# q and k transposed in float32 and split on the way out of PSUM, scores of two heads as 64-row tiles side by side, products with v in one piece

## The chip, the cores and the metric

The kernel is one program on one core of a Trainium2 chip. The metric is device time in microseconds (us) of one execution, from which medians over several runs are taken. Six instruction streams matter: TensorE (PE for matmuls, PEld for its weight loads), VectorE (DVE), ScalarE (ACT), GpSimd (POOL) and SyncE (SP), which here only issues DMAs. Each stream runs its instructions in program order; streams wait for each other through semaphores.

## What is computed

Attention with a learned bias, and behind it a mixture of experts. Cut to what matters here (B = 8, H = 8, S = 576, D = 64):

```python
scores = (1 / sqrt(D)) * np.matmul(q, k.transpose(0, 1, 3, 2))
psi_rel = np.log1p(np.abs(pos[:, None] - pos[None, :]))
x = (psi_rel / np.log1p(np.maximum(pos[:, None], 1.0)))[..., None]
bias = np.maximum(x @ w1 + b1, 0.0) @ w2              # S x S x H
scores = scores + bias.transpose(2, 0, 1)[None]
attn = np.exp(scores - scores.max(-1)); attn = attn / attn.sum(-1)
x = np.matmul(attn, v)                                # then, per token:
e = argmax(x @ w_gate + modality_bias); y = gate * (relu(x @ w1[e]) @ w2[e])
```

The matrix products have to be nearly float32. The kernel gets this from fast products of a reduced type (F32R) by splitting a number into a high part (its value rounded to F32R) and a low part (the rest), and adding the products high·high, low·high and high·low.

## The kernel before

**Stages.** First a table of the bias is made (`bias_table`, with `bias_hidden`, `bias_out`, `bias_put`): 36 blocks, each a hidden layer on DVE or ACT, a matmul with `w2` on PE, a scaling on the way out of PSUM, and DMAs that lay the rows out in `NBm` (query rows below 512) and `NBr` (the last 64). The last four blocks (`bias_late`) run inside the first pair of heads, and their rows go to `NBr` in 32 DMAs (L211). `first_steps` puts the preparation of pair 0 and 1 between the blocks. Then comes attention, and then the experts' tiles (from about 700 us on), which the change does not touch.

**Attention** goes through 32 pairs of heads (`attention`, L566), one pair after the other, and each pair through five steps u = 0 to 4. Step u handles the query rows of chunk u (128 rows of each head for u below 4; for u = 4 the last 64 rows of both heads together). What each step issues, and in which order, stands in the five strings of `ORDER` (L558): each letter is a piece of work, and since no scheduler reorders anything, the letters set the order on every engine at once.

- `S` (`scores`): the products of a chunk of q with all 576 keys, into one of two PSUM tiles `sps` (one per head); behind it on DVE one custom instruction (L435) that adds the bias, finds the minimum and writes `E`. Before, one `S` is one head of a chunk ("slot"): 128-row matmuls, in which the 128 rows hold high and low part of q over the 64 dimensions, four of 288 columns each. The scores come out negated.
- `e`, `f` (`exps`): exp of head 0 and head 1 on ACT, in place in `E`.
- `t`, `T` (`etrans`): four PE transposes each of `E` of the chunk two steps earlier (head 0, head 1) into PSUM `eps`, and the copy out to `eT` by `take` (on ACT for the names in `ON_ACT`, otherwise on DVE).
- `C` (`compact`, POOL) and `R` (`rtrans`): the last 64 keys of each chunk, copied together and transposed into `rT`.
- `a A` and `b c` (`av`): products of v with `eT` for query half 0 and half 1 of the pair before, each half in two parts; the second part adds the product for the last 64 keys (L517) and copies out to `xTb` on ACT.
- `k q` (`split`, POOL): high and low part of q and k in SBUF, side by side in the free dimension. `0` to `4` (`prep`): PE transposes of these, so that high parts land in rows 0 to 63 and low parts in rows 64 to 127 of `QT` and `KT`, and the copies out. `W` (`swap`): two DMAs that write `QT` once more with its halves exchanged. `K` (`heads`): four DMAs that put the parts for u = 4 into `KH` and `QD`. `L`, `V`: loads for later pairs.
- `X`, `B`: steps of the routing of the batch before, on PE and other engines.

All DMAs of this stage but the routing's scatters stand in one queue in the order of SP's instructions.

## Time and profile before

| | us |
|---|---|
| runs | 1196.64, 1191.96, 1195.97; median 1195.97 |
| the profiled execution | 1198.66 |
| its span, from first to last instruction | 1196.7 |
| first score matmul / last score matmul | 71.1 / 698.4 |
| PE busy in the span | 1132.1 |
| ACT / DVE / POOL busy in the span | 728.3 / 754.1 / 383.7 |

The page of the profile gives busy times and the costliest groups, each line of kernel.py with its engine, the tiles it writes and reads, the count, the busy time, and the idle time just before with what ended it. The timeline gives instructions in order of time: start, duration, engine, line, operation, how many were merged into the row, and in square brackets the idle time before the row with its releaser. A row of windows gives the busy time of each engine in a stretch, then the clock granted to TensorE (1.00 is full), the share of the DMA engines and GB/s. All times count from the start of the span.

### The profile page before, as it was taken

The page shows a single profiled execution, that of the slowest core. Times are in us where ns is not written, and L with a number is a line of the kernel's source. Part 1 is how long each engine was busy: PE and PEld are TensorE (multiplying, and loading weights), DVE is VectorE, ACT ScalarE, POOL GpSimd, SP SyncE. Part 2 cuts the span into 40 slices and gives each one's busy share as a digit, 9 for nine tenths or more (in the row PEclk, how much of TensorE's full clock was granted, in tenths as well). Part 3 has the DMA queues.
Part 4 walks back from the last instruction along what each step waited for, and adds up shares of the span by engine and source line. Part 5 has one row for each costly group of instructions (what it writes and reads, how often), then busy time and mean ns, then how long its engine had stood idle before and what let it go on. Part 6 is the DMA issues. An engine that isn't in the chain of part 4 may idle for free. (4 is left out here: it accounts for less than half of the span.)

```text
span 1196.7 us, 23090 instructions
## 1 busy us (share of the span) xinstructions
PE 1132.1 (95%) x8202; PEld 919.5 (77%) x8202; DVE 754.1 (63%) x1552; ACT 728.3 (61%) x1412; POOL 383.7 (32%) x525
## 2 busy tenths in 40 slices
PE   7977999899999899999998979999999999999997
PEld 3445777667778577777776758988899899989975
DVE  7974567457666475666757637577555645664667
ACT  5565667657767477677775654545545645554566
POOL 2203223434435325444353323532221123122122
PEclk9998999999999999999999999999999999999999
DMA  6854433764745635555365560221113314311361
GB/s 173 192 121 126 112 95 102 115 94 111 125 96 126 98 93 125 113 121 125 93 116 111 162 108 10 72 67 37 45 55 115 107 45 144 113 45 48 121 244 33
DMA packets 91311, 124.26 MB, mean 104 GB/s; under 512 B 35697, under 2 KB 60657, under 8 KB 91188
## 3 DMA queue, kind: packets, MB, share of 16 engines
q1 hardware_dynamic: 83188, 101.35, 36.3%
q0 software_dynamic: 8000, 21.35, 5.9%
q8 instruction: 68, 1.11, 0.5%
q14 instruction: 55, 0.45, 0.1%
HBM read 140.09 MB, written 19.90 MB: 134 GB/s over the span
## 5 line engine op out<-in xcount | busy, mean ns | idle before, releaser
L435 DVE CUSTOM_DVE_ANT_0 Eb<-sps,NBm 128x576 f32<-128x576 f32 x256 | 190.1, 755 | 183.8 <-PE sps L420 93.7
L449 ACT ACTIVATE Eb<-Eb,mn 128x576 f32<-128x576 f32 x288 | 221.5, 770 | 40.5 <-DVE mn L435 36.7
L420 PE MATMUL sps<-KT,QT 128*128 128x288 f32 x1152 | 222.7, 319 | 22.0 <-DMA QT<-QT 21.1
L420 PEld LDWEIGHTS sps<-KT,QT 128*128 128x128 f32 x1152 | 166.5, 191 | 27.4 <-issue 22.3
L1144 PE MATMUL p<-QT,w1hi 128*128 128x256 f32 x1152 | 163.9, 285 | 5.2 <-ACT w1hi L1117 5.2
L463 PE MATMUL eps<-idf,Eb 128*128 128x128 f32 x1024 | 159.9, 282 | 0.6 <-DVE lgs L781 0.3
L507 PE MATMUL xps<-eT,vraw 128*64 128x288 f32 x1024 | 155.0, 425 | 1.5 <-DVE QT L1129 1.0
L1144 PEld LDWEIGHTS p<-QT,w1hi 128*128 128x128 f32 x1152 | 150.8, 194 | 7.3 <-ACT w1hi L1117 6.1
L463 PEld LDWEIGHTS eps<-idf,Eb 128*128 128x128 f32 x1024 | 114.9, 142 | 39.5 <-issue 29.5
L1170 POOL DMA_INDIRECT out<-mo,idt x36 | 51.8, 1440 | 291.1 <-ACT mo L1169 262.6
L1147 DVE SCALAR_TENSOR_TENSOR hl<-p,hh 128x512 fp32r<-128x512 f32 x72 | 49.7, 690 | 138.9 <-ACT hh L1146 134.6
L454 POOL COPY rem<-Eb 128x128 f32<-128x128 f32 x128 | 37.5, 297 | 252.3 <-ACT Eb L449 245.1
L309 ACT ACTIVATE eT<-eps 128x512 f32<-128x512 f32 x192 | 111.4, 591 | 9.5 <-PE eps L463 8.7
L1161 PE MATMUL p<-w2lo,hh 128*128 128x512 f32 x288 | 112.9, 392 | 3.5 <-DVE w2lo L1111 2.2
L1111 DVE TENSOR_TENSOR w2lo<-NBm,w2hi 128x1024 fp32r<-128x1024 f32 x81 | 98.7, 1224 | 24.9 <-ACT w2hi L1110 24.8
L1161 PE MATMUL p<-w2hi,hh 128*128 128x512 f32 x288 | 114.0, 396 | 0.0
L1161 PE MATMUL p<-w2hi,hl 128*128 128x512 f32 x288 | 112.5, 391 | 0.0
L1146 ACT ACTIVATE hh<-p 128x512 fp32r<-128x512 f32 x72 | 43.1, 598 | 111.2 <-PE p L1144 103.1
L309 ACT ACTIVATE xTb<-xps 128x288 f32<-128x288 f32 x64 | 26.4, 412 | 122.9 <-PE xps L517 118.8
L507 PEld LDWEIGHTS xps<-eT,vraw 128*64 128x64 f32 x1024 | 63.1, 138 | 46.6 <-issue 12.6
L1111 DVE TENSOR_TENSOR w1lo<-NBm,w1hi 128x1024 fp32r<-128x1024 f32 x84 | 97.9, 1227 | 0.0
L1144 PE MATMUL p<-QT,w1lo 128*128 128x256 f32 x576 | 93.4, 285 | 0.3 <-DVE w1lo L1118 0.3
(227 smaller groups left out, 1991.3 us busy)
## 6 DMA issues: line engine op xcount, KB each, us to landing
NBm<-moe_w SPq DMA_DIRECT2D x24, 2048.0 KB
NBm<-moe_w SPq DMA_DIRECT2D x46, 1024.0 KB
QT<-QT SPq DMA_DIRECT2D x64, 304.0 KB
NBm<-xTb SPq DMA_DIRECT2D x32, 288.0 KB
KH<-KT SPq DMA_DIRECT2D x64, 144.0 KB
qraw<-q SPq DMA_DIRECT2D x32, 256.0 KB
kraw<-k SPq DMA_DIRECT2D x32, 256.0 KB
vraw<-v SPq DMA_DIRECT2D x32, 256.0 KB
```

The costliest lines, as they stand in the source:

```text
L309: self.nc.scalar.activation(out, ps, AF.Copy, scale=scale)
L420: nc.tensor.matmul(ps[:, half, :], q, k[:, HS * half : HS * half + HS], start=i == 0, stop=i == len(terms) - 1, skip_group_check=True,)
L435: nc.vector.tensor_tensor_reduce(out=e.rearrange("p (t w) -> p t w", t=2), in0=ps, in1=nb.rearrange("p (t w) -> p t w", t=2), scale=1.0, s ...
L449: self.nc.scalar.activation(e, e, AF.Exp, bias=mn, scale=-1.0, accum_out=sm)
L463: nc.tensor.transpose(ps[:, k, :], e[:, part, P * k : P * k + P], self.idf)
L507: nc.tensor.matmul(ps[o, :], v[:, h, k, :], self.eT[:, h, k, sl], start=k == 0, stop=False, tile_position=(0, 64 * h), skip_group_check=True,)
L1111: (lo or self.nc.vector).tensor_tensor(l, w, h.bitcast(F32), op=ALU.subtract)
L1144: nc.tensor.matmul(ps[:, a, :], w[:, c, fs], x[:, c, :], start=i == 0, stop=i == len(ops) - 1)
L1146: nc.scalar.activation(hh[:, sl, :], ps, AF.Relu)
L1147: nc.vector.scalar_tensor_tensor(hl[:, sl, :], ps, 0.0, hh[:, sl, :].bitcast(F32), op0=ALU.max, op1=ALU.subtract)
L1161: nc.tensor.matmul(ps, h[:, f, sl], m[:, f, :], start=i == 0, stop=i == len(ops) - 1)
L1170: nc.gpsimd.indirect_dma_start(out=self.out, out_offset=IndirectOffsetOnAxis(ap=ids, axis=0), in_=o, in_offset=None, bounds_check=self.n_t ...
```

## The change

**q and k.** The POOL split, the F32R identity and the DMAs `W` and `K` go. `prep` now transposes the raw float32 q and k, both heads side by side (head 0 lands in rows 0 to 63, head 1 in rows 64 to 127), four 128x128 transposes for q (`0`), four for k (`1`) and two small ones for the last 64 rows (`2`), instead of 18. Out of PSUM, ACT writes the high part and DVE then subtracts it from the PSUM value and writes the low part, so `QT` and `KT` hold the high parts in plane 0 and the low parts in plane 1. `D` copies the block-diagonal `QD` on POOL. The loads of q and k bring the heads of a chunk next to each other, in pieces of 64 numbers.

**Scores.** One `S` now does both heads of a chunk. For each of three terms (high·high, low·high, high·low) and each half of the keys it issues two matmuls of 64 rows, head 0 at array rows 0 to 63 and head 1 at rows 64 to 127, into two different PSUM tiles: 12 matmuls where two slots had 8. u = 4 keeps six 128-row matmuls.

**v.** `a A` and `b c` stand together, and the copies out are letters of their own (`y`, `z`).

**Order.** The strings of `ORDER` are rewritten. **Bias.** The last 64 rows are grouped another way, with a small table `tg1` of their own, so that `NBr` is written by 8 DMAs instead of 32.

```diff
@@ bias_put
-            for cg in range(4):
-                for par in range(2):
-                    r0 = 64 * par + 4 * cg + c
-                    nc.sync.dma_start(self.NBr[r0 : r0 + 49 : 16, :, :], o[32 * cg + par : 32 * cg + 32 : 2, :])
+            r0 = 16 * (blk - NMAIN)
+            for par in range(2):
+                nc.sync.dma_start(self.NBr[64 * par + r0 : 64 * par + r0 + 16, :, :], o[par:P:2, :])
@@ qk_loads
-            nc.sync.dma_start(
-                t[:, 0:8, :].rearrange("p (h c) d -> p h (c d)", h=2),
-                src[:, 0:512, :].rearrange("h (p c) d -> p h (c d)", c=4),
-            )
+            for h in range(2):
+                nc.sync.dma_start(t[:, h:8:2, :], src[h, 0:512, :].rearrange("(p c) d -> p c d", c=4))
+                yield
+            nc.sync.dma_start(t[0:64, 8:10, :], src[:, 512:S, :].rearrange("h r d -> r h d"))
             yield
-            for h in range(2):
-                nc.sync.dma_start(t[64 * h : 64 * h + 64, 8, :], src[h, 512:S, :])
-                yield
@@ prep
+        raws = (self.qraw[n], self.kraw[n])
+        if part < 2:
+            for c in range(4):
+                x = raws[part][:, 2 * c : 2 * c + 2, :].rearrange("p h d -> p (h d)")
+                nc.tensor.transpose(ps[:, P * c : P * c + P], x, self.idf)
         else:
+            for j, x in enumerate(raws):
+                x = x[0:64, 8:10, :].rearrange("p h d -> p (h d)")
+                nc.tensor.transpose(ps[:, 64 * j : 64 * j + 64], x, self.idf[0:64, 0:64])
...
         def out():
+            for j in (0, 1) if part == 2 else (part,):
+                cols = slice(512, S) if part == 2 else slice(0, 512)
+                p = ps[:, 64 * j : 64 * j + 64] if part == 2 else ps
+                T = (QT, KT)[j]
+                hi, lo = T[:, 0, cols], T[:, 1, cols]
+                if j == 0:
+                    nc.scalar.activation(hi, p, AF.Copy, scale=sc)
+                    nc.vector.scalar_tensor_tensor(lo, p, sc, hi.bitcast(F32), op0=ALU.mult, op1=ALU.subtract)
+                else:
+                    nc.scalar.copy(hi, p)
+                    nc.vector.tensor_tensor(lo, p, hi.bitcast(F32), op=ALU.subtract)
-    def swap(self, n):
...
     def heads(self, n):
-            self.nc.sync.dma_start(KH[o, :], KT[0:64, h, :])
-            self.nc.sync.dma_start(QD[o, o], QT[0:64, 0, 512 + P * h : 576 + P * h])
+            self.nc.gpsimd.tensor_copy(self.QD[o, :, o], QT[o, 0:2, 512:S].bitcast(F32))
@@ scores
+        sps = [t[:, :, 0:HS] for t in self.sps]
+        terms = ((0, 0), (1, 0), (0, 1))
+        for i, (a, b) in enumerate(terms):
             for half in range(2):
+                k = KT[:, b, HS * half : HS * half + HS]
+                kw = dict(start=i == 0, stop=i == len(terms) - 1, skip_group_check=True)
+                if u == 4:
+                    nc.tensor.matmul(sps[1][:, half, :], self.QD[:, a, :], k, **kw)
+                    continue
+                for h in range(2):
+                    o = slice(64 * h, 64 * h + 64)
+                    q = QT[o, a, P * u : P * u + P]
+                    nc.tensor.matmul(sps[h][:, half, :], q, k[o], tile_position=(64 * h, 0), **kw)
@@ av
-        if part == 1:
-            self.take(f"av{half}", self.xT[n][:, sl], ps)
+    def av_out(self, n, half):
+        self.take(f"av{half}", self.xT[n][:, HS * half : HS * half + HS], self.avps[half][:, 0:HS])
@@ ORDER
-        "S R S e f k X T a t B C",
-        "L S 1 A t e S 4 f 0 C T",
-        "t S S e f b q C T",
-        "B S c e S T 3 2 t f W C V",
-        "S X X e K T B X t",
+        "S R T e X t f B C",
+        "L S T e a A t y f 0 D C",
+        "S t e T f 1 C",
+        "B S e b c T z f 2 t C V",
+        "S X X e T B X t",
```

The change in three places, in the order in which instructions stand on an engine. On DVE, from the last bias instruction of u = 1 on in one pair; L435 is the scores' instruction (its second row reads the minimum out), `QT` and `KT` from L313 and L311 are copies out of `prep`, `eT` from L311 those of the transposed `E`. Before:

```order
L435 ISA Eb,mn_3_1253<-sps_750,NBm 128x576
L435 ISA mn_3_1253 128x1
L313 TENSOR_SCALAR QT_73<-xps_78 128x2x64
L313 TENSOR_SCALAR QT_73<-xps_77 128x512
L435 ISA Eb,mn_4_1279<-sps_749,NBm 128x576
L435 ISA mn_4_1279 128x1
L435 ISA Eb,mn_5_1285<-sps_750,NBm 128x576
L435 ISA mn_5_1285 128x1
L311 COPY eT<-eps_752 128x4x128
L435 ISA Eb,mn_6_1306<-sps_749,NBm 128x576
```

With the change the same place reads as follows (L418 is the scores' instruction, L378 and L381 write the low parts of q and k, L314 is `take`):

```order
L418 ISA Eb,mn_11_1196<-sps_728,NBm 128x576
L418 ISA mn_11_1196 128x1
L378 SCALAR_TENSOR_TENSOR QT_73<-xps_77,QT_73 128x512
L418 ISA Eb,mn_20_1240<-sps_727,NBm 128x576
L418 ISA mn_20_1240 128x1
L418 ISA Eb,mn_21_1242<-sps_728,NBm 128x576
L418 ISA mn_21_1242 128x1
L314 COPY eT<-eps_730 128x4x128
L381 TENSOR_TENSOR KT_105<-xps_78,KT_105 128x512
L418 ISA Eb,mn_30_1276<-sps_727,NBm 128x576
```

The instructions ahead of the scores of u = 2 and u = 3 now read `QT` and `KT` as well as PSUM: they come behind ACT's copy of the high part, not behind PE alone.

On ACT at the same place (L449 exp, L309 `take`), before:

```order
L309 ACTIVATE xTb_94<-xps_78 128x288
L309 ACTIVATE eT<-eps_751 128x4x2x64
L449 ACTIVATE Eb,sums_1184<-Eb,mn_2_1230 128x576
L309 ACTIVATE KT_109<-xps_78 128x2x64
L449 ACTIVATE Eb,sums_1184<-Eb,mn_3_1253 128x576
L309 ACTIVATE rT<-eps_752 128x64
```

and with the change, from the exp of u = 1, head 0, on (L433 exp, L312 `take`, L377 the high part of q):

```order
L433 ACTIVATE Eb,sums_1150<-Eb,mn_10_1194 128x576
L312 ACTIVATE eT<-eps_729 128x4x2x64
L312 ACTIVATE xTb_94<-xps_78 128x288
L433 ACTIVATE Eb,sums_1150<-Eb,mn_11_1196 128x576
L377 ACTIVATE QT_73<-xps_77 128x512
L312 ACTIVATE eT<-eps_729 128x4x128
```

The high part of q is new on ACT and stands behind the copies of `eT` and `xTb` and behind the exp of head 1.

On PE, around the products with v for half 0 of one pair (L463 and L469 transposes of `E`, L507 and L517 products with v, L369 transposes of q), before:

```order
L463 MATMUL eps_752<-idf,Eb 128x128 x4
L507 MATMUL xps_78<-eT,vraw_1346 64x288 x4
L463 MATMUL eps_751<-idf,Eb 128x128 x4
L420 MATMUL sps_749<-KT_108,QT_72 128x288 x4
L369 MATMUL xps_77<-idr,qs 128x128 x4
L507 MATMUL xps_78<-eT,vraw_1346 64x288 x4
L517 MATMUL xps_78<-rT,vrem_117 128x288
L469 MATMUL eps_751<-idf,Eb 128x128 x4
L420 MATMUL sps_750<-KT_108,QT_72 128x288 x4
```

and with the change, from the last score matmul of u = 1 to the first of u = 2 (L409 scores, L458 and L453 transposes of `E`, L491 and L501 products with v, L363 transposes of q):

```order
L409 MATMUL sps_728<-KT_105,QT_73 128x288
L458 MATMUL eps_730<-idf,Eb 64x64 x2
L491 MATMUL xps_78<-eT,vraw_1115 64x288 x8
L501 MATMUL xps_78<-rT,vrem_109 128x288
L453 MATMUL eps_729<-idf,Eb 128x128 x4
L363 MATMUL xps_77<-idf,qraw_1174 128x128 x4
L409 MATMUL sps_727<-KT_105,QT_73 128x288
```

The two parts of a half stand together with nothing between, and score matmuls, which before lay between them, come before and behind.

More of the change, by code (lines that the diff above doesn't have):

```diff
@@ L41 @@
 NBLK = S4 // 4
-X0 = 131
-TW = X0 + S4
+X0, X1 = 115, 15
+TW, TW1 = X0 + S4, X1 + S4
 def bias_base(blk, cg):
@@ L53, in bias_base @@
         return o + 16 * cg + 64 * half, c
-    return P + cg, blk - NMAIN
+    return P + 4 * (blk - NMAIN) + cg, 0
 def bias_rows(blk, cg):
     s, c = bias_base(blk, cg)
-    return [4 * (s + 4 * g) + c for g in range(4)]
+    return [4 * (s + 4 * g) + c if blk < NMAIN else 4 * s + g for g in range(4)]
 def n_tiles(n_tok):
@@ L274, in attn_early @@
         self.rt = right(name="rt", bufs=1)
-        self.idr = cp.tile([P, P], F32R, name="idr")
-        nc.scalar.copy(self.idr, self.idf)
         self.eT = cp.tile([P, 2, 4, S], F32, name="eT")
         self.rT = cp.tile([P, S], F32, name="rT")
-        self.qs = cp.tile([P, 9, 2, D], F32R, name="qs")
-        self.ks = cp.tile([P, 9, 2, D], F32R, name="ks")
         self.KT = [cp.tile([P, 2, S], F32R, name=f"KT{k}") for k in range(2)]
-        self.KH = cp.tile([P, S], F32R, name="KH")
-        self.QD = cp.tile([P, P], F32R, name="QD")
+        self.tg1 = cp.tile([P, 4, TW1], F32, name="tg1")
+        self.QD = cp.tile([P, 2, P], F32R, name="QD")
         nc.gpsimd.memset(self.QD.bitcast(F32), 0.0)
@@ L349, in load_v @@
         self.vmain[n] = t
-    def split(self, n, part):
-        x = (self.qraw, self.kraw)[part].pop(n)
-        xs = (self.qs, self.ks)[part]
-        self.nc.gpsimd.tensor_copy(xs[:, :, 0, :], x)
-        self.nc.gpsimd.tensor_tensor(xs[:, :, 1, :], x, xs[:, :, 0, :].bitcast(F32), op=ALU.subtract)
     def prep(self, n, part):
@@ L364, in prep @@
         ps = self.xbank()
-        pr = ps.bitcast(F32R).rearrange("p (j w) -> p j w", j=4)
-        if part < 4:
-            xs = (self.qs, self.ks)[part // 2]
-            for j in range(4):
-                nc.tensor.transpose(
-                    pr[:, j, :], xs[:, 4 * (part % 2) + j, :, :].rearrange("p a d -> p (a d)"), self.idr
-                )
-        else:
-            for j, xs in enumerate((self.qs, self.ks)):
-                nc.tensor.transpose(pr[:, j, :], xs[:, 8, :, :].rearrange("p a d -> p (a d)"), self.idr)
+        raws = (self.qraw[n], self.kraw[n])
@@ L407, in scores @@
+    def scores(self, n, u):
         nc = self.nc
-        b, p = divmod(n, NP)
+        p = n % NP
         QT, KT = self.QT[n % 2], self.KT[n % 2]
-        ps = self.sps[slot % 2 if slot < 8 else 1][:, :, 0:HS]
-        if slot < 8:
-            c, h = divmod(slot, 2)
-            o = (704 if h else 0) + P * c
-            terms = [(QT[:, sw, o : o + P], KT[:, h, :]) for sw in range(2)]
-        else:
-            c = 4
-            terms = [(QT[:, 1, 512 + 64 * h : 640 + 64 * h], KT[:, h, :]) for h in range(2)] + [(self.QD, self.KH)]
@@ L418, in scores @@
-        for i, (q, k) in enumerate(terms):
-            for half in range(2):
-                nc.tensor.matmul(
-                    ps[:, half, :],
-                    q,
-                    k[:, HS * half : HS * half + HS],
-                    start=i == 0,
-                    stop=i == len(terms) - 1,
-                    skip_group_check=True,
-                )
-        if slot == 0:
-            self.sums[n] = self.smp.tile([P, 9], F32, tag="sums", name=f"sums{n}", bufs=8)
-        if slot in (0, 2, 4, 6, 8):
-            self.E[n, c] = self.Eb[:, next(self.e_next)]
@@ L432, in scores @@
-        e = self.E[n, c][:, slot % 2, :]
-        nb = self.NBm[:, 8 * c + 2 * p + slot % 2, :] if slot < 8 else self.NBr[:, p, :]
-        mn = self.smp.tile([P, 1], F32, tag="mn", name=f"mn{n}_{slot}", bufs=4)
-        nc.vector.tensor_tensor_reduce(
-            out=e.rearrange("p (t w) -> p t w", t=2),
-            in0=ps,
-            in1=nb.rearrange("p (t w) -> p t w", t=2),
-            scale=1.0,
-            scalar=3.0e38,
-            op0=ALU.add,
-            op1=ALU.min,
-            accum_out=mn,
-        )
@@ new lines, in scores @@
+        if u == 0:
+            self.sums[n] = self.smp.tile([P, 9], F32, tag="sums", name=f"sums{n}", bufs=8)
+        self.E[n, u] = self.Eb[:, next(self.e_next)]
+        found = []
+        for h in range(2 if u < 4 else 1):
+            e = self.E[n, u][:, h, :]
+            nb = self.NBm[:, 8 * u + 2 * p + h, :] if u < 4 else self.NBr[:, p, :]
+            mn = self.smp.tile([P, 1], F32, tag="mn", name=f"mn{n}_{u}{h}", bufs=4)
+            nc.vector.tensor_tensor_reduce(
+                out=e.rearrange("p (t w) -> p t w", t=2),
+                in0=sps[h if u < 4 else 1],
+                in1=nb.rearrange("p (t w) -> p t w", t=2),
+                scale=1.0,
+                scalar=3.0e38,
+                op0=ALU.add,
+                op1=ALU.min,
+                accum_out=mn,
+            )
+            found.append((e, mn, self.sums[n][:, 2 * u + h : 2 * u + h + 1]))
@@ L537, in first_steps @@
         add(0, lambda: self.load_v(0))
-        add(2, lambda: self.split(0, 0))
-        add(4, lambda: self.split(0, 1))
-        for blk, k in zip(self.PREP0, (0, 1, 4, 2, 3)):
+        for blk, k in zip(self.PREP0, range(3)):
             add(blk, lambda k=k: pe(k))
             add(blk + 1, lambda k=k: evac.pop(k)())
-        add(self.SWAP0, lambda: self.swap(0))
-        add(self.HEADS0, lambda: self.heads(0))
         if self.n_pair > 1:
```

66 lines of the change are left out of this document (30 added, 36 removed).

## Prediction

> **What bounds the kernel now.** I read the page first, then windows over the attention stage, then the waits of PE there, then the timeline of one pair.
>
> ```profile
> PE 1132.1 (95%) x8202; PEld 919.5 (77%) x8202; DVE 754.1 (63%) x1552; ACT 728.3 (61%) x1412; POOL 383.7 (32%) x525
> ```
>
> The average says PE. The windows say how strictly: two stretches of four pairs (one batch) each.
>
> ```profile
> 448.14:522.82 74.68, 74.34 (x588) 58.58 (x588) 48.66 (x132) 53.01 (x127) 32.44 (x53) 1.00 0.52 116
> 522.82:597.50 74.68, 74.33 (x588) 58.56 (x588) 48.69 (x132) 53.01 (x127) 32.43 (x53) 1.00 0.52 116
> ```
>
> The columns are PE, PEld, DVE, ACT, POOL, the clock, the DMA share, GB/s. Both take 74.68 us to the last digit, PE is busy all but 0.34 us, the clock is full: a quiet pair takes 74.68 / 4 = **18.67 us** and PE alone sets it. ACT has 53.0 of 74.7 us, DVE 48.7. Outside such stretches PE waits:
>
> ```profile
> PE sps L420 <- DMA QT<-QT: 21.1, 4, 13.9
> PE xps L374 <- POOL ks L356: 4.2, 2, 3.0
> PE xps L491 <- POOL rem L454: 3.6, 1, 3.6
> PE xps L491 <- issue: 1.5, 1, 1.5
> ...
> 60.00:100.00 40.00, 24.14 (x233) 16.64 (x230) 23.09 (x57) 20.46 (x43) 5.13 (x8) 0.85 0.55 133
> ...
> 226.00:232.00 6.00, 4.08 (x33) 3.07 (x31) 2.23 (x5) 3.88 (x10) 3.63 (x7) 1.00 0.64 131
> 236.00:246.00 10.00, 7.02 (x38) 5.36 (x37) 3.42 (x9) 4.29 (x12) 4.38 (x7) 0.66 0.74 88
> 408.00:420.00 12.00, 9.16 (x65) 6.30 (x65) 2.79 (x9) 4.79 (x10) 4.06 (x9) 0.86 0.40 91
> 636.00:646.00 10.00, 6.78 (x47) 4.56 (x48) 7.45 (x28) 4.12 (x10) 4.12 (x9) 0.83 0.56 124
> 678.00:688.00 10.00, 7.93 (x50) 6.39 (x52) 2.75 (x8) 5.40 (x12) 4.16 (x7) 0.83 0.48 137
> ```
>
> The first four rows are waits of PE from 60 to 735 us (total, times, longest). The windows show what each long one costs besides: the clock falls behind it. A window's loss is its length by one minus the clock: 6.0 us, 0, 3.4, 1.7, 1.7 and 1.7.
>
> **Stalls that the change takes away.** The longest is the first, between pair 0 and 1:
>
> ```profile
> 71.22 13.25 SPq L211 DMA_DIRECT2D NBr<-xTb  x23
> 83.95 5.67 SPq L211 DMA_DIRECT2D NBr<-xTb  x10
> 98.26 0.82 PE L420 MATMUL sps<-KT,QT 128*128 128x288 f32 x2 [13.91 <-DMA QT<-QT]
> ```
>
> SP issues 32 small DMAs for `NBr` in 18.4 us (0.57 each), only then the loads and the swap that pair 1 waits for. Eight issues of the same kind are about 8 x 0.6 = 5 us from 72 on, over before PE's wait began at 84 (98.26 - 13.91), and no swap is left. So 21.1 us of waits for swaps and 4.2 us for POOL's split go, and with them the clock losses behind them, 6.0 + 3.4 + 1.7 + 1.7 = 12.8 us: **38 us**. The two waits for `rem` (5.1 us, and 1.7 of clock) may stay: POOL still stands behind the routing's scatters. POOL loses its split, but a lap with less slack (below) will feel the scatters more often, for which I give back 4. Net **34 us**.
>
> **PE's own work in a pair.** All from one pair, by starts of groups:
>
> ```profile
> 488.13 0.66 PE L463 MATMUL eps<-idf,Eb 128*128 128x128 f32 x4
> 488.72 1.19 PE L507 MATMUL xps<-eT,vraw 128*64 128x288 f32 x8
> 489.84 0.66 PE L463 MATMUL eps<-idf,Eb 128*128 128x128 f32 x4
> 490.25 0.78 PE L420 MATMUL sps<-KT,QT 128*128 128x288 f32 x4
> 490.53 0.60 ACT L309 ACTIVATE eT<-eps 128x512 f32<-128x512 f32 x1 [0.33 <-PE eps L463]
> ...
> 491.20 0.76 DVE L435 CUSTOM_DVE_ANT_0 Eb<-sps,NBm 128x576 f32<-128x576 f32 x1 [2.31 <-ACT eT L309]
> ...
> 492.38 0.75 PE L517 MATMUL xps<-rT,vrem 128*128 128x288 f32 x2
> 492.96 0.60 PE L469 MATMUL eps<-idf,Eb 128*128 128x128 f32 x4
> ...
> 495.15 1.10 PEld L420 LDWEIGHTS sps<-KT,QT 128*128 128x128 f32 x8
> 495.18 1.30 PE L420 MATMUL sps<-KT,QT 128*128 128x288 f32 x8
> ...
> 501.25 0.89 PE L369 MATMUL xps<-idr,ks 128*128 128x128 f32 x8
> 501.96 0.63 PE L463 MATMUL eps<-idf,Eb 128*128 128x128 f32 x4
> ```
>
> A 288-column score matmul: eight weight loads in 1.10, (1.10 - 0.19) / 7 = 0.13 us each, and 0.133 fits the matmuls. A transpose of float32 takes 0.109 (L469: four in 0.60 with the last lasting 0.27), so four 0.44; one of F32R (0.71 / 8) 0.089. A v step, both heads' records side by side: 1.19 for four, the last lasting 0.43, first one slow, so 0.243. From 488.13 to 490.25 are 2.12 us; two times 0.44 and 4 x 0.243 are 1.85, so going into column tiles and out again costs 0.27, about 0.145 a change. L517 takes 0.58, 0.68 with the change before it.
>
> Scores: 32 matmuls x 0.133 = 4.26 us give way to 24 steps of two matmuls. That two 64-row tiles run side by side no row shows; the nearest is the pair of column tiles in L507. I take 0.133 a step: 3.19, so 1.07 less. Bounds: 0.12 (a tenth less) and 0.266 (one after the other). Transposes: 18 x 0.089 = 1.6 to about 1.1, 0.5 less. Changes of tile: before there are five segments of column tiles in a pair (a, A, b, c and the small transposes L474), ten changes; after, four row segments and two column segments of which two pairs touch, again ten. v in one piece thus gains nothing by itself, it pays for the score tiles. PE's work falls by 1.5 us, to 17.1 with routing, 16.1 without (routing steps are about 1 us a pair). By PE alone that is 32 x 1.5 = 48 us.
>
> **What is late next.** In the new order each low part waits on DVE for ACT's high part, and the scores' instruction queues behind it. Hops, from these rows and the ones above:
>
> ```profile
> 496.09 0.76 DVE L435 CUSTOM_DVE_ANT_0 Eb<-sps,NBm 128x576 f32<-128x576 f32 x1 [0.27 <-issue]
> ...
> 496.77 0.75 DVE L435 CUSTOM_DVE_ANT_0 Eb<-sps,NBm 128x576 f32<-128x576 f32 x1
> ...
> 498.30 0.69 DVE L311 COPY eT<-eps 128x512 f32<-128x512 f32 x1 [0.76 <-PE eps L463]
> ...
> 498.90 0.75 DVE L435 CUSTOM_DVE_ANT_0 Eb<-sps,NBm 128x576 f32<-128x576 f32 x1
> ...
> 500.56 0.41 ACT L309 ACTIVATE xTb<-xps 128x288 f32<-128x288 f32 x1 [2.04 <-PE xps L517]
> ...
> 500.87 0.77 ACT L449 ACTIVATE Eb<-Eb,mn 128x576 f32<-128x576 f32 x1
> ...
> 501.63 0.59 ACT L309 ACTIVATE eT<-eps 128x512 f32<-128x512 f32 x1
> ...
> 502.17 0.60 ACT L309 ACTIVATE KT<-xps 128x512 fp32r<-128x512 f32 x1
> ...
> 503.56 0.76 DVE L435 CUSTOM_DVE_ANT_0 Eb<-sps,NBr 128x576 f32<-128x576 f32 x1 [0.17 <-ACT Eb L449]
> ...
> 504.36 0.78 ACT L449 ACTIVATE Eb<-Eb,mn 128x576 f32<-128x576 f32 x1 [0.83 <-DVE mn L435]
> ```
> ```profile
> 801.41 0.60 ACT L1146 ACTIVATE hh<-p 128x512 fp32r<-128x512 f32 x1 [2.14 <-PE p L1144]
> ...
> 802.04 0.69 DVE L1147 SCALAR_TENSOR_TENSOR hl<-p,hh 128x512 fp32r<-128x512 f32 x1 [5.23 <-ACT hh L1146]
> ```
>
> Last transpose to ACT's copy: end of the group + 0.2. End of scores to DVE: about 0.3 (490.25 plus four steps, 491.20); I take 0.27. DVE's scores instruction holds DVE 0.68 (496.09 to 496.77), frees PSUM after 0.82, and lets exp start after 0.80. Exp holds ACT 0.76 (500.87 to 501.63), a 512-column copy 0.5, an `xTb` copy 0.31 (500.56 to 500.87), a 64-column one 0.1 (an estimate by size). High part to low part 0.63 (the last two rows, the same pair of instructions in the experts), 64 columns 0.25 by size. A low part or an `eT` copy holds DVE 0.61; a small low part 0.17.
>
> Now one lap, from the scores of u = 3 to those of the next pair, always along what comes last. S 0.8; change and b c 2.1; last keys 0.68; T 0.44: 4.0. Then ACT: 0.2, copy of `eT` 0.5, `xTb` 0.31, exp of head 1 0.76, the small high parts, then DVE's two small low parts: at 6.4. Only then comes DVE's copy of the `eT` that frees `eps` for `t` of u = 4: 0.74, at 7.1, where PE would have been ready at 5.9: a stall of **1.2**. t 0.44, S of u = 0 after the PSUM of u = 4's scores is read: 7.8; S 0.8, 0.27, two reads on DVE 0.68 + 0.82: S of u = 1 at 10.4 (PE alone 10.2). S 0.8, change 0.15, L458 0.2, a A 1.94, last keys 0.68, t 0.44: 14.6. Then ACT again: 0.2, `eT` 0.5, `xTb` 0.31, exp of head 1 0.76, high to low part of q 0.63, low part 0.61, and only then the two reads of u = 2's scores, 0.68 + 0.82: S of u = 3 at **19.1**, PE alone 17.6, a stall of **1.5**. With 0.2 for the routing steps that are not inside a stall: **19.3 us** a pair, 0.63 more than now, though PE has 1.5 less to do. 32 x 0.63 = 20.
>
> Lying beside other work: the added ACT copies (about 0.7 us a pair) and the DVE change count only where the lap has them. `D` on POOL stands three steps ahead of u = 4; uncovered it would put off the six matmuls of u = 4 by its own length, some tenths. The loads of q and k in smaller pieces are issued more than a pair ahead; late, they would stall PE at `0`. The bias stage gets a 6% smaller first table behind the same DVE work; I count 0 (one more load and one scaling, 0 to 1 us).
>
> **The sum**, against the profiled execution of 1198.66 (2.7 above the median of 1195.97): 1198.7 + 20 - 34 = **1184**.
>
> [...] The rows before the change have ACT and DVE at 71% and 65%, so neither is full; what they show is order, not load.
>
> **Rivals.**
> - *PE stays the bound.* If ACT and DVE run further ahead than I have it, the lap is 17.1 or 17.2: 1198.7 - 47 - 34 = **1117**. For it: PE has not waited for either in the quiet stretches. Against: the orders on ACT and DVE leave no way past. Chance 0.15.
> - *Two weight loads a step.* The loads of both heads go one after the other at 0.085 to 0.089, the spacing of the F32R transposes, so 0.17 to 0.18 a step instead of 0.133. Three S on the lap x 6 x 0.037 = 0.7 us, 22 us in all: **1206**. Against: L420's loads lie wholly beside the matmuls. Chance 0.15. [...]
> - *Slower: the 64-row tiles run one after the other*, 0.266 a step: 3 x 6 x 0.133 = 2.4 us a lap, 77 us: **1260**. It decides the sign: with the 34 us of stalls a pair may grow by 1.06, 0.43 more than the lap has, so above 0.133 + 0.43 / 18 = 0.157 a step the kernel is slower. For it: no row has such tiles. Against: L507's column tiles start together. Chance 0.10.
> - *The clock falls in the new stalls.* After a wait of 1.9 us (226 to 232) it stayed at 1.00, after 2.1 (678 to 688) it fell. Mine are 1.2 and 1.5; if one a pair reached 2, 1.7 us each, up to 54 us more, **1215 to 1238**. Chance 0.08.
>
> **How the numbers follow.** The forecast has 0.52, with 1165 to 1205 of its own (half a microsecond a lap either way, 16, and 5 on the stalls). What this kernel's measurement can tell from no change is about 0.5%, 6 us. Faster: most of the forecast (0.40) and PE as bound, 0.55. Same: 0.18, from the forecast's upper end and the weight loads. Slower: 0.27. The range 1115 to 1215 takes in the first rival and the second, and leaves out the last two.
>
> **What would show it.** A pair in a quiet stretch at 19.3 (17.2: PE bound; 20 and more: the tiles). PE waits of 1.5 us ahead of L409 for DVE and of 1.2 ahead of L447 for L314. Score matmuls of the two heads starting within 0.01 us, steps 0.133 apart. No wait above 3 us between 80 and 100, the clock 1.00 in 60 to 100. Wrong it would be if ACT's copies after L453 came sooner than 0.2 behind it, or if SP's shorter queue let something else be late.

## The result, and the profile after

The changed kernel is **slower**: 1229.38 us median (1228.31 to 1230.81, 4 runs) against 1194.47 (1191.96 to 1196.64, 4 runs) of the kernel before on the same chip, ratio 1.0294 with a 95% interval of 1.0267 to 1.0321. The prediction was 1184, with 1115 to 1215 as its range. The profiled execution took 1228.75 us, so the forecast, which was made against a profiled execution of 1198.66, missed by 45 us.

Windows of the changed kernel: a quiet batch of four pairs, a pair without routing, and the end of the bias table with the first pairs of attention, columns as before.

```profile
514.95:596.41 81.46, 74.08 (x619) 54.19 (x619) 46.47 (x131) 54.74 (x135) 18.26 (x44) 1.00 0.24 60
...
108.09:127.53 19.44, 17.28 (x145) 12.84 (x146) 9.90 (x25) 12.85 (x33) 1.69 (x6) 1.00 0.18 45
...
60.00:100.00 40.00, 34.41 (x339) 22.30 (x334) 27.70 (x70) 29.67 (x65) 2.98 (x11) 1.00 0.62 125
```

A quiet batch takes 81.45 us where it took 74.68. PE's busy time in it is the same to 0.3 us (74.08 against 74.34), but PE now idles 7.4 us of it. PE has stopped being the bound, as forecast, but with as much to do as before, which was not forecast. From 60 to 100 us the clock is 1.00 (0.85 before): the long first stall is gone.

Who ends PE's waits, from 60 to 740 us (total, times, longest):

```profile
PE sps L409 <- DVE mn L418: 38.9, 83, 1.7
PE xps L818 <- DVE KT L381: 9.6, 13, 0.9
PE sps L404 <- POOL QD L390: 9.3, 2, 6.2
PE eps L447 <- DVE eT L314: 6.4, 11, 1.4
PE xps L748 <- DVE KT L381: 3.8, 7, 0.5
PE xps L818 <- DVE base L801: 3.4, 7, 0.5
```

No DMA stands there any more. The first row is mostly u = 3's scores waiting for DVE's reads of u = 2's, once for each head. The second and fifth are routing steps that wait for a PSUM bank until DVE has written the low part of k. The fourth is the forecast wait ahead of u = 4's second transposes. One lap in the timeline shows both places:

```profile
96.09 0.60 ACT L377 ACTIVATE QT<-xps 128x512 fp32r<-128x512 f32 x1
...
96.72 0.69 DVE L378 SCALAR_TENSOR_TENSOR QT<-xps,QT 128x512 fp32r<-128x512 f32 x1 [4.08 <-ACT QT L377]
...
97.33 0.75 DVE L418 CUSTOM_DVE_ANT_0 Eb<-sps,NBm 128x576 f32<-128x576 f32 x1
...
98.14 0.40 PE L409 MATMUL sps<-KT,QT 64*128 64x288 f32 x1 [0.74 <-DVE mn L418]
...
98.82 1.06 PE L409 MATMUL sps<-KT,QT 64*128 64x288 f32 x11 [0.28 <-DVE mn L418]
...
104.68 0.22 ACT L377 ACTIVATE QT<-xps 128x64 fp32r<-128x64 f32 x1
...
104.93 0.23 DVE L378 SCALAR_TENSOR_TENSOR QT<-xps,QT 128x64 fp32r<-128x64 f32 x1 [2.64 <-ACT QT L377]
105.19 0.21 ACT L380 CAST KT<-xps 128x64 fp32r<-128x64 f32 x1 [0.29 <-DVE QT L378]
105.44 0.22 DVE L381 TENSOR_TENSOR KT<-xps,KT 128x64 fp32r<-128x64 f32 x1 [0.28 <-ACT KT L380]
105.58 0.68 DVE L314 COPY eT<-eps 128x512 f32<-128x512 f32 x1
...
106.31 0.66 PE L447 MATMUL eps<-idf,Eb 128*128 128x128 f32 x4 [1.14 <-DVE eT L314]
```

Read it as a chain. DVE idles 4.08 us until ACT has written the high part of q, writes the low part, and only then reads u = 2's scores, for which PE waits at 98.14 and, for the second head, at 98.82. Six microseconds on, high and low parts of the last 64 rows of q and k go ACT, DVE, ACT, DVE, each waiting for the one before; the copy of `eT` and with it `t` come behind. The row of 11 matmuls in 1.06 us also settles a rival: 64-row tiles of the two heads do run side by side (1.06 / 5.5 is at most 0.19 us a step, where 0.266 was priced for one tile after the other).

The third row of the waits is POOL's doing:

```profile
241.61 0.97 POOL L840 DMA_INDIRECT tab<-ids,pos  x1 [7.48 <-DMA tab<-ids,pos]
...
242.82 0.29 POOL L390 CAST QD<-QT 64x128 fp32r<-64x128 f32 x1
249.62 0.29 POOL L390 CAST QD<-QT 64x128 fp32r<-64x128 f32 x1 [6.51 <-DMA tab<-ids,pos]
```

Of the two copies into `QD` the second starts 6.51 us late, when the scatter issued at 241.61 has landed. The list of POOL's instructions in the built program, with their waits, shows why: the second copy, and not the first, has a wait of its own for a scatter's DMA (DMASW is a scatter's semaphore):

```
L840 DMA tab<-ids,pos_4837 36992x1 [waits DMASW1_49]
...
L390 CAST QD<-QT_72 64x2x64 [waits PE_49]
L390 CAST QD<-QT_72 64x2x64 [waits DMASW2_49,Pool_49]
```

Where the time went, by windows from the first scores' instruction of pair 0 to that of pair 31, the kernel before in the first row, the changed one in the second:

```profile
72.75:681.94 609.19, 574.85 (x4479) 451.09 (x4472) 381.03 (x1022) 405.18 (x965) 232.01 (x375) 0.98 0.52 112
```
```profile
72.42:714.40 641.98, 569.05 (x4728) 414.74 (x4721) 361.31 (x1022) 419.41 (x1027) 126.60 (x316) 0.99 0.27 60
```

This stretch has 27 pairs beside which the routing of an earlier batch runs, 3 without, and pair 0. The laps by quiet rates are 27 x 18.67 + 3 x 17.39 = 556.3 before, which leaves 52.9 for pair 0 and all stalls; after, 27 x 20.36 + 3 x 19.45 = 608.1, which leaves 33.9. So **laps cost 52 us more, stalls 19 less**; what lies behind the stretch is 2 us shorter. Forecast were 20 and 34.

### The profile page after: what moved, and what is told of

Its sections match the earlier page's. It is cut to its first block, busy times and chain, and to the rows that moved or that the text cites. A ratio compares the mean times of both kernels' runs of the same rounds, so it can differ in the third digit from the quotient of the medians.

```text
span 1227.0 us, 23058 instructions
## 1 busy us (share of the span) xinstructions
PE 1118.2 (91%) x8458; PEld 879.6 (72%) x8458; DVE 726.5 (59%) x1551; ACT 741.4 (60%) x1475; POOL 273.2 (22%) x461
## 5 line engine op out<-in xcount | busy, mean ns | idle before, releaser
L433 ACT ACTIVATE Eb<-Eb,mn 128x576 f32<-128x576 f32 x288 | 223.4, 776 | 127.9 <-DVE mn L418 126.4
L418 DVE CUSTOM_DVE_ANT_0 Eb<-sps,NBm 128x576 f32<-128x576 f32 x256 | 182.7, 751 | 41.3 <-PE sps L409 20.3
L409 PE MATMUL sps<-KT,QT 64*128 64x288 f32 x1536 | 157.3, 312 | 38.9 <-DVE mn L418 38.9
L409 PEld LDWEIGHTS sps<-KT,QT 64*128 64x128 f32 x1536 | 117.3, 184 | 73.6 <-DVE mn L418 59.6
L447 PE MATMUL eps<-idf,Eb 128*128 128x128 f32 x1024 | 149.9, 280 | 7.1 <-DVE eT L314 6.4
L312 ACT ACTIVATE eT<-eps 128x512 f32<-128x512 f32 x192 | 114.0, 595 | 63.0 <-PE eps L453 42.7
L378 DVE SCALAR_TENSOR_TENSOR QT<-xps,QT 128x512 fp32r<-128x512 f32 x64 | 29.3, 458 | 198.8 <-ACT QT L377 189.4
L491 PE MATMUL xps<-eT,vraw 128*64 128x288 f32 x1024 | 136.8, 409 | 0.7 <-ACT eT L312 0.7
L491 PEld LDWEIGHTS xps<-eT,vraw 128*64 128x64 f32 x1024 | 68.0, 137 | 44.0 <-issue 5.1
```

The costliest lines, as they stand in the source:

```text
L312: self.nc.scalar.activation(out, ps, AF.Copy, scale=scale)
L409: nc.tensor.matmul(sps[h][:, half, :], q, k[o], tile_position=(64 * h, 0), **kw)
L418: nc.vector.tensor_tensor_reduce(out=e.rearrange("p (t w) -> p t w", t=2), in0=sps[h if u < 4 else 1], in1=nb.rearrange("p (t w) -> p t w" ...
L433: self.nc.scalar.activation(e, e, AF.Exp, bias=mn, scale=-1.0, accum_out=sm)
L447: nc.tensor.transpose(ps[:, k, :], e[:, part, P * k : P * k + P], self.idf)
L491: nc.tensor.matmul(ps[o, :], v[:, h, k, :], self.eT[:, h, k, sl], start=k == 0, stop=False, tile_position=(0, 64 * h), skip_group_check=True,)
```

## The experiments

The theory: the order on ACT and DVE (a low part that waits for a high part, and what queues behind it) sets the lap, and POOL's waits for scatters the stalls. The rival: PE's own work with 64-row tiles and changes of tile. The experiments ran on other chips, where the kernel before took 1218 to 1222 us; what compares is therefore the ratio of each kernel to the kernel before on the same chip, beside the quiet laps.

| kernel | median us | before there | ratio, 95% interval | pair without routing, us |
|---|---|---|---|---|
| c_after (the changed kernel) | 1251.54 | 1217.87 | 1.0250 (1.0205 to 1.0294) | 19.44 |
| e1b_nbr32 | 1263.69 | 1220.0 | 1.0336 (1.0274 to 1.0399) | 19.47 |
| e2_order | 1206.24 | 1220.0 | 0.9860 (0.9804 to 0.9917) | 16.76 |
| e3_hipair | 1249.23 | 1220.0 | 1.0206 (1.0145 to 1.0267) | 19.18 |
| e4_heads | 1239.48 | 1220.0 | 1.0157 (1.0094 to 1.0221) | 19.46 |
| e5_qd_dve | 1180.18 | 1221.98 | 0.9642 (0.9591 to 0.9692) | 16.77 |
| e6_scat | 1159.72 | 1221.98 | 0.9477 (0.9429 to 0.9524) | 16.75 |
| e7_u1u2 | 1223.94 | 1221.98 | 1.0021 (0.9992 to 1.0050) | 18.48 |
| e8_u3 | 1255.76 | 1221.98 | 1.0279 (1.0220 to 1.0338) | 18.87; 20.34 at clock 0.92 |
| e9_rem_act | 1149.84 | 1217.87 | 0.9424 (0.9385 to 0.9463) | 16.53 |
| e10_rem_dve | 1157.92 | 1217.87 | 0.9489 (0.9450 to 0.9528) | 17.04 |
| e11_x | 1273.84 | 1219.13 | 1.0422 (1.0335 to 1.0509) | 19.44 |
| e12_tx | 1264.78 | 1222.32 | 1.0369 (1.0287 to 1.0451) | 19.43 |

**The changed kernel again** (c_after).

> The changed kernel once more, word for word, beside the versions built from it. Theory A: the ratio to the kernel before is a matter of order and comes out at 1.024 to 1.036, with quiet laps of 19.45 us. Theory B (the loss hangs on this or that chip's scatters): outside of that, with the laps as they were.

The ratio, 1.0250 (1.0205 to 1.0294), is the first chip's within the intervals, and the lap is the same to 0.02 us. What differs between the traces of the two chips are the stalls: the pair at 228 us took 28.16 on the first chip, 33.95 here, and PE's waits for `QD`, 9.3 us there, are here (total, times, longest):

```profile
PE sps L404 <- POOL QD L390: 27.0, 6, 11.9
```

**The order of the preps** (e2_order).

```diff
-        "L S T e a A t y f 0 D C",
-        "S t e T f 1 C",
-        "B S e b c T z f 2 t C V",
+        "L S T e f 0 a A t y D C",
+        "S 1 t e T f C",
+        "B S 2 e f b c T z t C V",
```

> The changed kernel with three strings of ORDER rewritten: prep 0, 1 and 2 each go some letters earlier, so that PE has a transposition or products of v between a high part and what waits behind its low part; the exp of head 1 goes ahead of evacuations. No instruction is added or taken away. Theory A (the order on ACT and DVE sets the lap of 19.45 us): PE becomes the bound at 16.8 to 17.3 us in a pair without routing and about 18 with it, in all 1145 to 1165 us, 65 to 85 less than the changed kernel. Theory B (the 64-row tiles and changes of tile make PE's own work longer): the lap stays above 19, less than 10 us of difference.

A pair without routing, in the windows:

```profile
104.14:120.90 16.76, 16.76 (x145) 12.86 (x146) 9.99 (x25) 12.67 (x33) 1.69 (x6) 1.00 0.23 55
```

PE is busy all of it, at 16.76 us: with the same instructions in another order PE is the bound again, and the lap is 2.7 us shorter. For the lap the theory holds and the rival falls. The total is 3.9% of the kernel before, 48 us, below the changed kernel instead of the 65 to 85 expected, because the stalls grew:

```profile
PE sps L404 <- POOL QD L390: 50.0, 8, 13.7
```

50 us of waits of u = 4's scores for `QD`, against 27.0 in c_after. That a shorter lap leaves less room for the same scatters fits this, but no run tests it by itself.

**One half of the order at a time** (e7_u1u2, e8_u3).

```diff
 e7_u1u2
-        "L S T e a A t y f 0 D C",
-        "S t e T f 1 C",
+        "L S T e f 0 a A t y D C",
+        "S 1 t e T f C",
 e8_u3
-        "B S e b c T z f 2 t C V",
+        "B S 2 e b c T z f t C V",
```

> The changed kernel with the strings of u = 1 and u = 2 of e2_order alone (preps of q and k earlier, exp of head 1 ahead of the evacuations), u = 3 as it was. Theory A (each stall of the lap stands for itself): the wait of 1.45 us ahead of u = 3's scores goes, the one of 1.14 ahead of u = 4's transposes stays; a pair without routing 18.0 us, against 19.45 of the changed kernel. Theory B (one engine is as long as the lap, so what one stall loses the next takes up): above 19.0.

> The changed kernel with prep 2 at the start of u = 3 instead of in front of its last transposes, all else as it was. Theory A: the wait of 1.14 us ahead of u = 4's transposes and the 0.34 us of the high part of k go, the one of 1.45 ahead of u = 3's scores stays; a pair without routing 17.9 to 18.1 us; a pair with routing falls by 1.5 to 2.3, since the bank of prep 2 is free before the routing's steps in u = 4 want it. Theory B: above 19.0 without routing.

With the first two strings alone a pair takes 18.48: the wait ahead of u = 3's scores is gone, the one ahead of u = 4's transposes (1.13) is still there. The fall is 0.96, about the 0.74 + 0.28 that the timeline shows at that place, not the 1.45 that I had put down by also counting part of the first matmul. The third string alone is a miss, and its pairs without routing do not agree among themselves. The first two, and PE's waits in the kernel (total, times, longest):

```profile
85.98:104.85 18.87, 16.73 (x146) 12.71 (x145) 9.73 (x24) 12.34 (x32) 1.71 (x7) 1.00 0.17 41
...
106.07:126.41 20.34, 18.20 (x145) 13.38 (x146) 10.00 (x26) 12.77 (x33) 1.69 (x6) 0.92 0.19 46
```
```profile
PE sps L409 <- DVE mn L418: 36.5, 74, 1.7
PE xps L491 <- DVE KT L381: 33.6, 30, 1.1
```

At full clock a pair takes 18.87, 0.58 less than in the changed kernel. The second has the same waits, but the clock falls behind them, and 16 products of v take 3.60 us instead of 2.16:

```profile
99.53 2.16 PE L491 MATMUL xps<-eT,vraw 128*64 128x288 f32 x16 [1.12 <-DVE KT L381]
...
118.44 3.60 PE L491 MATMUL xps<-eT,vraw 128*64 128x288 f32 x16 [1.12 <-DVE KT L381]
```

A quiet batch with routing takes 80.62 at full clock (581.69 to 662.31), against 81.45, and the ratio, 1.0279, cannot be told from c_after's.

The new row of waits is the products of v, 1.1 us in each of 30 pairs. The preps, the products of v and the routing take turns in two PSUM banks. With prep 2 moved ahead of `b c`, `b` gets the bank in which prep 1 still waits for its low part on DVE. Moved together, as in e2_order, prep 1 is done by then: no wait of `b` for `KT` stands among PE's there. So the two halves of the new order do not simply add up (0.96 and 0.58 alone, 2.7 together): with two banks in turn, each prep of this kernel needs its low part out before the next but one user.

**High parts first** (e3_hipair): the small instructions of prep 2 as high q, high k, low q, low k.

```diff
...
+            for j in js:
                 if j == 0:
-                    nc.scalar.activation(hi, p, AF.Copy, scale=sc)
-                    nc.vector.scalar_tensor_tensor(lo, p, sc, hi.bitcast(F32), op0=ALU.mult, op1=ALU.subtract)
+                    nc.scalar.activation(hi[0], p[0], AF.Copy, scale=sc)
                 else:
-                    nc.scalar.copy(hi, p)
-                    nc.vector.tensor_tensor(lo, p, hi.bitcast(F32), op=ALU.subtract)
+                    nc.scalar.copy(hi[1], p[1])
+            for j in js:
+                if j == 0:
+                    nc.vector.scalar_tensor_tensor(lo[0], p[0], sc, hi[0].bitcast(F32), op0=ALU.mult, op1=ALU.subtract)
+                else:
+                    nc.vector.tensor_tensor(lo[1], p[1], hi[1].bitcast(F32), op=ALU.subtract)
```

> The changed kernel, with the four small instructions behind prep 2 issued as high q, high k, low q, low k instead of high q, low q, high k, low k. Theory A (the high part of k waits on ACT for the low part of q on DVE, since both read one PSUM tile and the order is kept, 0.3 us a pair on the lap): 31 x 0.34 = 10 us less, -7 to -12. Theory B (something else ends last there): within 3 us of the changed kernel.

The lap fell by 0.27, from 19.45 to 19.18, 8 us in 31 pairs; the ratios, 1.0250 and 1.0206, differ by 5 us, which lies within their intervals. By the lap, the wait of the high part of k for the low part of q is on the path; the total alone would not show it.

**QD earlier** (e4_heads), **and on DVE** (e5_qd_dve, on top of e2_order).

```diff
 e4_heads
-        "S R T e X t f B C",
-        "L S T e a A t y f 0 D C",
+        "D S R T e X t f B C",
+        "L S T e a A t y f 0 C",
 e5_qd_dve (against e2_order)
-        "S R T e X t f B C",
-        "L S T e f 0 a A t y D C",
+        "S D R T e X t f B C",
+        "L S T e f 0 a A t y C",
-            self.nc.gpsimd.tensor_copy(self.QD[o, :, o], QT[o, 0:2, 512:S].bitcast(F32))
+            self.nc.vector.tensor_copy(self.QD[o, :, o], QT[o, 0:2, 512:S].bitcast(F32))
```

> The changed kernel with D, the two POOL copies into QD, one step earlier: at the start of u = 0 instead of in u = 1. Theory A (the long waits at 250 and 418 us are u = 4's scores waiting for QD, which stands behind scatters that are issued in u = 0): -8 to -13 us. Theory B (POOL is late whichever copy comes first, and the small-key copies wait in D's place): -4 to 0.

> As e2_order, with the two copies D into QD on DVE at the start of u = 0 instead of on POOL in u = 1. Theory A (the long waits of u = 4's scores come from POOL: its second copy into QD has a wait of its own for the scatter before it): the quiet laps of 16.76 us stay, the waits of 3 to 14 us ahead of u = 4's scores go, and of the 61 us that e2_order's pairs had over its quiet laps 35 to 60 go; 0.94 to 0.957 of the kernel before. Theory B (POOL is late as a whole and the copies of the last keys, which also stand on it, wait instead): less than 20 us, 0.97 or more.

e4_heads is 0.9% of the kernel before, or 11 us, below c_after, as forecast, though the intervals overlap. PE's waits for `QD` are 2.4 us in its trace (27.0 in c_after, on another chip), and 7.7 us of waits for `rem` came in. e5_qd_dve is 2.2%, 27 us, below e2_order, between what the two theories gave. PE's waits in it say why it was not more:

```profile
PE xps L475 <- POOL rem L438: 16.6, 5, 5.7
```

The waits for `QD` are gone, but the copies of the last keys (`C`, the tile `rem`), which also stand on POOL, have taken their place in part: `R` waits for them.

**Scatter behind C, C on another engine** (e6_scat on top of e5_qd_dve, the next two on top of e6_scat).

```diff
 e6_scat
-        "B S 2 e f b c T z t C V",
+        "S 2 e f b c T z t C V B",
 e9_rem_act / e10_rem_dve
-        self.nc.gpsimd.tensor_copy(t, self.E[n, c][:, :, 512:S])
+        self.nc.scalar.copy(t, self.E[n, c][:, :, 512:S])           (e10: nc.vector.tensor_copy)
```

> As e5_qd_dve, with the scatter step of u = 3 moved from the start of u = 3 behind the copy of the last keys. Theory A (what is left of the stalls is that copy behind a scatter that waits for the scatter before it): 0 to 15 us less than e5_qd_dve, and no wait above 2 us at the small-key transposes between 140 and 680 us. Theory B (nothing is left there): within 3 us of e5_qd_dve.

> As e6_scat, with the copies of the last keys (C) on ACT, right behind the exp whose result they take, instead of on POOL. Theory A (the 6.2 and 2.1 us that PE waits at 233 and 382 us in e6_scat are the scores' instruction waiting to overwrite E until POOL, behind a scatter, has copied from it): both go, with the clock behind them 8 to 11 us less, 0.936 to 0.942 of the kernel before; ACT has room for the 1 to 1.5 us a pair, and the quiet lap stays at 16.76. Theory B (ACT's order is too tight for it): the quiet lap passes 17.0, and the kernel is no faster than e6_scat.

> As e9_rem_act, but the copies of the last keys on DVE. They wait there for ACT's exp of head 1 with the next scores' reads behind them. Theory A (a wait of DVE for ACT at the end of each step is covered, since PE needs 0.8 us and more for the next scores): quiet lap 16.76, time as e9_rem_act within 3 us. Theory B (it is what the changed kernel suffers from, once more): quiet lap 17.5 or more, slower than e6_scat by 15 us or more.

e6_scat is 20 us below e5_qd_dve, more than expected, and no wait at its small-key transposes is left among PE's longest. e9_rem_act is the fastest of all, **0.9424 of the kernel before (0.9385 to 0.9463)** and 8% below the changed kernel. Its windows: the stretch of 31 pairs and a pair without routing.

```profile
71.88:631.45 559.57, 543.00 (x4729) 410.17 (x4721) 376.86 (x1084) 442.87 (x1151) 74.75 (x131) 0.99 0.32 69
103.56:120.09 16.53, 16.53 (x146) 12.69 (x145) 10.35 (x27) 13.66 (x37) 0.00 (x0) 1.00 0.24 56
```

PE is busy 97% of the stretch (543.0 of 559.6 us; 569.1 of 642.0 in the changed kernel). The lap was expected to stay at 16.76 and is 16.53. A quiet batch takes 71.91 (502.91 to 574.82), where the kernel before took 74.68 with PE as the bound there too. The changed kernel's data path is thus worth having, with an order made for it and with the copies of `D` and `C` off POOL; what the kernel before would gain from moving its own copies and scatters was not tried. On DVE (e10_rem_dve) the lap is 17.04 and the kernel no faster than e6_scat, between the two theories. PE's one wait in that lap, 0.27, ends with a copy of `eT` on ACT; that DVE's wait for ACT's exp stands behind it is argued, not shown.

**Bias part undone** (e1b_nbr32): `NBr` by 32 DMAs from one table, as in the kernel before.

```diff
-            r0 = 16 * (blk - NMAIN)
-            for par in range(2):
-                nc.sync.dma_start(self.NBr[64 * par + r0 : 64 * par + r0 + 16, :, :], o[par:P:2, :])
+            for cg in range(4):
+                for par in range(2):
+                    r0 = 64 * par + 4 * cg + c
+                    nc.sync.dma_start(self.NBr[r0 : r0 + 49 : 16, :, :], o[32 * cg + par : 32 * cg + 32 : 2, :])
...
```

> The changed kernel with the bias part undone: one table again, and the last 64 rows written to NBr by 32 small DMAs instead of 8. Theory A (the first stall went because no swap is left in SP's queue): the loads of pair 2 are issued behind the 32 DMAs but are needed a pair later, so 0 to +3 us against the changed kernel. Theory B (it went because the 32 DMAs became 8): the wait of 10 to 14 us between pairs 0 and 1 comes back, +10 to +16 us.

The first wait comes back at a third of its size: SP's queue and PE's wait are

```profile
71.06 18.41 SPq L211 DMA_DIRECT2D NBr<-xTb  x32
```
```profile
92.51 1.80 PE L403 MATMUL sps<-KT,QT 64*128 64x288 f32 x11 [4.48 <-DVE mn L412]
```

PE waits 4.48 us here where the kernel before waited 13.91, and here it is DVE's scores' instruction that waits for `NBr`. DVE's wait for `NBr` is 4.70 us. The change of the bias and the lost swaps both have part in the stall that went; the first pair took 21.62 us here, 16.22 to 16.24 in the changed kernel, 26.46 before. That is 5.4 us, more than theory A and less than theory B had. The ratios of the whole kernels differ by 10 us, with intervals that overlap, and half of that lies outside the first pair.

**Routing steps elsewhere** (e11_x, e12_tx).

```diff
 e11_x
-        "S t e T f 1 C",
-        "S X X e T B X t",
+        "S t e T f 1 X C",
+        "S X e T B X t",
 e12_tx
-        "S X X e T B X t",
+        "S T e X X B X t",
```

> The changed kernel with one of the routing's three steps X of u = 4 moved to the end of u = 2, where PE waits 1.44 us for the reads of the scores in every pair. Theory A (the routing costs 0.93 us a pair, not 0.2, because its PE steps stand in u = 4 behind the bank of prep 2 and none lies in the larger stall of u = 3): a quiet batch falls from 81.45 to 78.5 to 79.8 us, 13 to 20 us in all. Theory B (the routing's own copies on DVE and ACT lengthen the order there as much as its PE steps fill): 80.5 us or more a batch, within 7 us of the changed kernel.

> The changed kernel with T of u = 4 ahead of the routing's two steps X instead of behind them. T's transposes use another PSUM tile, the routing's steps the bank that prep 2 holds until its low part of k is written. Theory A (a quiet batch has 0.54 + 0.91 + 0.48 + 0.54 us of waits for that bank, and what they put off behind them): T lies where PE waited, those waits shrink, and a quiet batch falls from 81.45 by 1.5 to 3.5 us, 10 to 25 us in all. Theory B (the same end of the lap, u = 4's second transposes behind DVE, is late whatever stands before it): within 0.8 us a batch.

In both theory A missed. A quiet batch at full clock took 83.16 in e11_x (334.83 to 417.99) and 81.89 in e12_tx (145.71 to 227.60), against 81.46, the first above the 80.5 of its theory B, the second within the 0.8 that its own allowed. The totals lie further off, 21 and 15 us above c_after by the ratios, the second with intervals that overlap.

In e11_x the extra step in u = 2 takes a turn of the two banks, and `b` waits for the bank of prep 1, as in e8_u3 (19 waits, 21.5 us). In e12_tx, PE's waits for the bank of prep 2 fell, but those for the bank of the routing step before rose in their place:

```profile
PE xps L818 <- DVE base L801: 9.1, 6, 1.5
...
PE xps L818 <- DVE KT L381: 2.9, 6, 0.5
```

(9.6, 13 times, and 3.4, 7 times, stood in the last and first row's place in the changed kernel.) With three routing steps in u = 4 going through two banks, a wait for a bank was there in both places of T; theory B's reason, `t` behind DVE, is not what rose.

## Why the prediction was wrong, point by point

Of the 45 us the laps have 32 (52 for a forecast of 20) and the stalls 15 (19 for 34); 2 come back behind the stretch.

**Right in its mechanism: what is late next.** Both stalls stand where the prediction put them (1.2 forecast and 1.14 found ahead of u = 4's transposes; 1.5 and 1.02 ahead of u = 3's scores), and e2_order removed both by order alone. The lap without routing was forecast at 19.1 and is 19.45. That it came so near is in part luck: PE works 17.28 of it where 16.1 was forecast, and the stalls are shorter by half a microsecond. Of the rivals, two weight loads a step (0.17 to 0.18) did not happen, since six steps with a change of tile take 0.99 us (last section), nor did tiles one after the other. A clock that falls in the new stalls did not happen in the changed kernel, whose quiet batches have 1.00; it did in e8_u3 (0.92 over a pair), behind waits of 1.12 us and less, where the prediction feared one of 2.

**The step that failed most: "with 0.2 for the routing steps that are not inside a stall".** A pair with routing takes 20.36, one without 19.45: 0.91 instead of 0.2, 27 x 0.7 = 19 us. The kernel before already had the size of these steps in its quiet pairs, 18.67 against 17.39, so 1.28 and not "about 1". They do lie where the stall ahead of `t` was: that wait is left in pairs 0 to 3, and 0.2 us of it once in a batch. But they bring a wait of their own, for the bank of prep 2: the rows "xps L818" and "xps L748 <- DVE KT" are 13.4 us over seven batches, and with "L818 <- DVE base" 16.8, 2.4 a batch or 0.6 a pair. 1.28 + 0.6 - 1.14 = 0.74 is most of the 0.91. That this wait is there, the trace shows; that it could have been avoided within this order, neither e11_x nor e12_tx showed.

**The next: "for which I give back 4".** The stalls, with pair 0, fell by 19 and not by 34 net. The kernel before lost less than was counted: of its 52.9 us, PE works 12.1 in pair 0 (first row below), so some 40 are stalls, where the prediction had 38 that go and 6.8 that stay. Most of the difference is the 6.0 us of clock behind the first wait. They were taken over a window that holds the wait itself, in which PE stands (0.00 busy at 0.62) and so loses nothing by the clock; the second row is that wait, the third what came behind it, which lost 13.74 x 0.12 = 1.6 us:

```profile
72.75:99.21 26.46, 12.11 (x110) 10.30 (x103) 11.19 (x29) 10.91 (x26) 5.13 (x8) 0.78 0.38 106
...
84.35:98.26 13.91, 0.00 (x1) 0.03 (x1) 1.37 (x3) 1.35 (x3) 4.55 (x6) 0.62 0.49 137
98.26:112.00 13.74, 13.74 (x94) 10.71 (x96) 6.76 (x17) 8.34 (x20) 2.86 (x5) 0.88 0.46 110
```

And the changed kernel's own stalls are larger than the 4 given back. Three first pairs of a batch in it, by windows:

```profile
146.98:167.04 20.06, 18.89 (x159) 13.62 (x160) 11.03 (x32) 13.13 (x34) 2.09 (x9) 1.00 0.12 29
228.44:256.60 28.16, 20.91 (x154) 14.31 (x153) 11.43 (x31) 13.09 (x32) 5.19 (x13) 0.88 0.24 42
...
399.64:423.84 24.20, 20.07 (x154) 13.46 (x153) 11.36 (x31) 13.18 (x33) 5.43 (x15) 0.93 0.38 54
```

Of the three the first is a quiet one; the others take 8.1 and 4.1 more. The prediction had `D` on POOL "uncovered" at "some tenths": it looked at the length of the copies, not at a wait of POOL ahead of them. Both long ones hold a wait for `QD`, 9.3 us in the two. e4_heads gives 11 us for it, within overlapping intervals, and e5_qd_dve shows what is behind it in the same queue. Pair 0 adds some 4 us more: in the changed kernel it already has the waits of the lap, and takes 16.22 us with 12.54 of work.

**A term left out of the lap: the high part of k.** The prediction's chain had "the small high parts, then DVE's two small low parts", as if ACT did its two without a pause. ACT waits 0.29 for DVE in between and DVE 0.28 for ACT behind it. e3_hipair: 0.27 a pair, 8 us. With it the forecast lap is 19.4.

**Wrong, but off the path: "PE's work falls by 1.5 us".** A lap of PE is 17.28 in the changed kernel (16.76 in e2_order's order) against 17.39: 0.1 to 0.6 less. The rows of the timeline show where the rest went, here one chunk of scores in e2_order:

```profile
104.55 1.04 PE L447 MATMUL eps<-idf,Eb 128*128 128x128 f32 x8
105.52 1.18 PE L409 MATMUL sps<-KT,QT 64*128 64x288 f32 x12
106.63 0.34 PE L458 MATMUL eps<-idf,Eb 128*64 128x64 f32 x4
```

From the start of eight transposes to the scores are 0.97 us, from there to the next group 1.11. In the kernel before:

```profile
503.76 1.04 PE L463 MATMUL eps<-idf,Eb 128*128 128x128 f32 x8
504.56 0.78 PE L420 MATMUL sps<-KT,QT 128*128 128x288 f32 x4
505.17 0.60 PE L491 MATMUL xps<-idf,rem 128*128 128x128 f32 x4
```

the same eight transposes take 0.80, one head's scores 0.61. So a chunk of both heads costs 0.97 + 1.11 = 2.08 now and about 0.80 + 2 x 0.61 = 2.02 then: the saving that was forecast, 0.27 a chunk, does not appear. At 0.109 a transpose and 0.133 a step, the prediction's own prices, the eight transposes and six steps are 0.87 + 0.80 = 1.67, so the two changes of tile at the edges take 0.41, about 0.2 each. The prediction balanced "ten" changes against "ten" at 0.145; going from 128-row transposes to 128-row scores had cost nothing by the same prices (0.87 + 0.53 = 1.40 against 0.80 + 0.61 = 1.41), so each change there is new and costs more than it counted, and prep 2's 64-row transposes are one more. Because the lap was set by ACT and DVE, none of this showed in the time; in the forecast for "PE stays the bound" (1117) it would have been 28 us and more.
